# Moving three value loads, four low parts of weights and the turn of one expert group's tokens in a fused attention and mixture-of-experts kernel

## Chip, cores and metric

The kernel runs on one core of a Trainium2 chip. The metric is the device time of one execution in microseconds (us); lower is better. A difference of under 1% is taken as no change.

## What is computed

A block-sparse attention is followed by a mixture of experts with one expert per token. The attention has 4 batches, 8 heads, 768 positions and 64 columns per head, in blocks of 32 positions. A block of queries sees its neighbours, the first and the last block, and three sampled blocks:

```
scores = where(mask, scale * q @ k.T, -1e9)
attn   = exp(scores - max) / (sum + 1e-9);  x = attn @ v        # 3072 tokens of 512
logits = x @ w_gate + modality_bias[modality_id];  e = argmax(logits)
out[e == i] = gate_w * (relu(x @ w1[i]) @ w2[i])                # w1 512x1024, w2 1024x512
```

Everything is float32. Products in the expert part are made of two parts: a number is kept as a rounded high part and the low part that is left (number minus high part), and a product is three matmuls: high by high, high by low, low by high.

## The kernel before

**Attention.** The queries of the first and last block are worked densely, all others in 22 tiles of 128 tokens (two halves of 11), each a batch pair with two blocks of queries. Tiles pass through a software pipeline whose steps are written out in order per engine (a manual schedule): scores (`scores`, L560), mask and maximum (L568), exponentials (L576), transposes (L585), copies to SBUF (`copied`, L590, tiles named `at`), sums over shared values (L607), sums over a tile's own sampled values (`weigh_own`, L616), division (`divide`, L461 to L463), and routing of the tokens (`turned`, `gate`, `route`, `rank`). The sampled values of a tile come by `fetch_own` (L548) with two calls of three loads of 128 KB each, issued on SP. `VG` holds where in the pipeline each call stands: the first at tick +9, place 6, the second at tick +10, place 3. `VS_SOON` and others place the copies of shared values (L530 on POOL).

**Experts.** Tokens are gathered by expert in groups of 256. There are twelve full groups and a half one here. Groups 0 and 1 are "early": they hold tokens of the first 16 and 18 tiles of 128 and run while attention ends (`early_groups`, a generator that is stepped once per part of a tick, so that its instructions are interleaved with the last attention work in a fixed order). A group has eight weights of 128x1024, numbered 8g to 8g+7; four for the first layer (`up`, L811 to L813, 96 matmuls), four for the second (`down`, L826 to L828, 48 matmuls). Each weight is loaded to a staging buffer (`fetch`, L738 to L745, on SP), rounded on ACT (L749), and its low part is made by one subtraction (`split`, L752) on VectorE (DVE), except for the numbers in `POOL_SPLITS`, which are made on GpSimd (POOL). There are five staging buffers, so weight n+5 can be fetched only when the low part of weight n is made. The first few weights of the early groups use three of the buffers only.

**Turning tokens.** A group's rows come by two indirect loads on POOL (`gather`, L763). They must be transposed, and split in high and low parts `xh`, `xl`. There are two ways. `column`, used for groups 0 to 2, turns two of the four columns per call with four TensorE transposes into PSUM (L770), then ACT copies the high part (L776) and DVE subtracts it from the PSUM tile (L777). From group 3 on the rows go another way: POOL takes the 16-bit halves of each number apart (`apart`, L786, two copies, after two tiny copies L781), SP issues one DMA transpose (`turn_halves`, L790), POOL puts the halves together again (`together`, L795, two copies), and `halve` makes the high part on ACT (L804, twice) and the low part on DVE (L805, twice) from SBUF. This way uses three buffers taken from the `at` tiles.

**Order around the change.** Each engine runs its instructions strictly in the order written. In the second layer of group 0, f counts from 0 to 7 and each f is two steps of the generator. Between these steps stand the last routing instructions on DVE (L316 to L389) and the chain that numbers all groups (`finish`, L1176 to L1238, then `rows_of`, L1077 to L1103), whose result L1079 releases the gathers of groups 2 and 3. `relu` (L818 on ACT, L819 on DVE) ends a first layer. `give` (L843 to L847) scales and scatters a group's output.

The columns of group 1 are turned by `columns(1)` at the end of f = 3 and f = 7.

Of the kernel before, what the change touches and what calls it, by code (L numbers as in the profile page):

```python
# [9 lines left out]
F32 = mybir.dt.float32  # L10
# [4 lines left out]
U16 = mybir.dt.uint16  # L15
# [6 lines left out]
P = 128  # L22
# [49 lines left out]
VS = (11, 7)  # L72
VS_SOON = (8, 7)
VG = ((9, 6), (10, 3))

DENSE_IN = ((19, 14, 30), (49, 38, 44))
Q_IN = 22
# [2 lines left out]
XD = (7, 7)  # L80
TAIL = 7
EVAC_DVE = ()
POOL_SPLITS = (7, 15, 16, 21)

TICKS = (6, 9, 12)
DOWN0 = ((9, 5), (9, 7), (14, 7), (12, 9), (13, 9), (13, 9), (17, 9), (15, 10))
# [5 lines left out]
def attention_moe(ctx, tc, kD, qD, qH, v0, v1, blocks, modality, w_gate, bias, w1, w2, out):  # L92
# [30 lines left out]
    with ExitStack() as actx:  # L123
# [623 lines left out]
        def split(n, eng=None, rest=None):  # L747
            h, l, s = wh[n % NRING], wl[n % NRING], staged(n)
            nc.scalar.copy(h, s)  # L749

            def low():
                (eng or (nc.gpsimd if n in POOL_SPLITS else nc.vector)).tensor_tensor(l, s, h.bitcast(F32), ALU.subtract)  # L752

            if rest is None:
                low()
            else:
                rest.append(low)
# [25 lines left out]
        def apart(g):  # L783
            keep_share(g, nc.gpsimd.tensor_copy)
            for t in range(2):
                nc.gpsimd.tensor_copy(halves[0][:, t * GT * 4:(t + 1) * GT * 4].rearrange("p (n f) -> p n f", n=2),  # L786
                                      xg[2 * (g % 2) + t][:, 0:HD].bitcast(U16).rearrange("p (f n) -> p n f", n=2))

        def turn_halves():
            nc.sync.dma_start_transpose(halves[1].rearrange("p (k r) -> p k r", r=P), halves[0])  # L790

        def together(g):
            bits = halves[2].rearrange("p (c t n) -> p n c t", n=2, t=GT)
            for t in range(2):
                nc.gpsimd.tensor_copy(bits[:, :, :, t * P:(t + 1) * P],  # L795
                                      halves[1][:, t * GT * 4:(t + 1) * GT * 4].rearrange("p (n c r) -> p n c r", n=2, c=4))

        def halve(g):
            whole = halves[2].bitcast(F32)
            for n in range(2):  # L800
                h = xh[g % 2][:, 2 * n:2 * n + 2, :].rearrange("p a b -> p (a b)")
                l = xl[g % 2][:, 2 * n:2 * n + 2, :].rearrange("p a b -> p (a b)")
                x = whole[:, n * 2 * GT:(n + 1) * 2 * GT]
                nc.scalar.copy(h, x)  # L804
                nc.vector.tensor_tensor(l, x, h.bitcast(F32), ALU.subtract)  # L805
# [46 lines left out]
        def early_groups():  # L852
            now = {"fetch": 0, "split": 0, "gather": 0, "column": 0, "half": 0}
            lows = []

            def load(nf, ns, slow=False):
                while True:
                    f, p = now["fetch"], now["split"]
                    if p < ns and p < f:
                        split(p, rest=lows if slow else None)  # L860
                        now["split"] += 1
                        if slow:
                            return
                    elif f < nf and f - NSTG < p and (f < 8 * NEAR or known):
                        if slow or now["half"]:
                            fetch(f, now["half"])
                            now["half"] ^= 1
                        else:
                            fetch(f)
                        now["fetch"] += not now["half"]  # L870
                        if slow:
                            return
                    else:
                        return

            def rows(g):
                if now["gather"] == g and ready[g] and (g != 1 or tail[1]) and (g or settled() and 2 * NM - 1 in shared):
                    if g == 1:
                        expert_slots(8)
                    gather(g)  # L880
                    if g == NEAR:
                        gather(g + 1)
                    now["gather"] += 1

            def columns(g):
                for n in range(2):
                    if now["column"] == 2 * g + n and now["gather"] > g:
                        column(g, n, bank())
                        now["column"] += 1
                        return  # L890

            expert_slots(0)
            tick, wait = 0, 0
            while not tail[0]:
                while lows:
                    lows.pop()()
                rows(0)
                if now["gather"]:
                    wait += 1
                    if wait > 8:  # L900
                        columns(0)
                p = sum(tick >= x for x in TICKS)
                load(p + 2, p, True)
                tick += 1
                yield "tick"
            while lows:
                lows.pop()()
            expert_slots(2, 5, 6, 7)
            while now["column"] < 2:
                rows(0)  # L910
                columns(0)
            load(10, 5)
            for k in range(4):
                o = bank()
                for c in range(4):
                    for f in (2 * k, 2 * k + 1):
                        up(0, c, f, o)
                    rows(1)
                    yield
                relu(k, o)  # L920
            o = [bank() for _ in range(2)]
            for f in range(8):
                load(*DOWN0[f])
                for t in range(2):
                    down(0, f, t, o[t])
                    rows(1)
                    yield
                if f in (3, 7):
                    columns(1)
            while not tail[1]:  # L930
                yield
            rows(1)
            for t in range(2):
                give(0, t, o[t])
            while now["column"] < 4:
                columns(1)
            o = [bank() for _ in range(4)]
            for c in range(4):
                load(*UP1[c])
                for f in range(8):  # L940
                    up(1, c, f, o[f // 2])
                    if f % 2:
                        rows(2)
                        yield
            for k in range(4):
                relu(k, o[k])
            turned_low.append(True)
            o = [bank() for _ in range(2)]
            for f in range(8):
                load(*DOWN1[f])  # L950
                for t in range(2):
                    down(1, f, t, o[t])
                    rows(2)
                    yield
                if f in (5, 6):
                    columns(2)
            while not ready[2]:
                yield
            rows(2)
            for _ in range(3):  # L960
                at_ = work.tile([P, 16, 2, 32], F32, name="at", bufs=NAT)
                halves.append(at_.rearrange("p a b c -> p (a b c)").bitcast(U16))
            apart(NEAR + 1)
            for t in range(2):
                give(1, t, o[t])
            load(22, 17)
            while now["column"] < 6:
                columns(2)
            load(22, 20)
# [307 lines left out]
        def side(t, f, place=7):  # L1277
            work_at.setdefault((t, place), []).append(f)
# [58 lines left out]
        for g in range(2 * NM):  # L1337
            half, m = divmod(g, NM)
            t = at["s", half, m, 0, 0]
            kl = lambda m=m, half=half: q_load(m, half)  # L1340
            qp = lambda m=m, half=half: share_k(m, half)
            vl = lambda m=m, half=half: fetch_v(m, half)
            vg = [lambda m=m, half=half, n=n: fetch_own(m, half, n) for n in range(2)]
            if g < 2:
                loads.update({f"kl{g}": kl, f"qp{g}": qp, f"vl{g}": vl, "vs1": lambda: share_v(1, 0), **{f"v{n}{g}": vg[n] for n in range(2)}})
                continue
            kt = last(g - 2) + KL[0]
            pt = max(kt, t + QP[0])
            vt = last(g - 2) + VL[0]
            side(kt, kl, KL[1])  # L1350
            side(pt, qp, QP[1])
            side(vt, vl, VL[1])
            if m:
                vs = VS_SOON if g >= 2 * NM - 2 else VS
                side(last(g - 2) + vs[0], lambda m=m, half=half: share_v(m, half), vs[1])
            for n in range(2):
                side(last(g - 2) + VG[n][0], vg[n], VG[n][1])

        st, done = {}, set()

# [164 lines left out]
```

## Time and profile before

| what | value |
| --- | --- |
| median of 3 runs | 528.4 us (523.78 to 529.88) |
| profiled execution | 526.72 us, its span 524.9 us |
| PE busy | 503.9 us, 96% of the span |
| DVE, ACT, POOL busy | 388.5, 336.8, 285.5 us |
| HBM traffic | 225 GB/s over the span |

Busy time of an engine counts its instructions, not the waits. "PE" is TensorE's matmuls, "PEld" its weight loads, "SPq" the queue of SyncE, from which nearly all loads are issued. In a row of a timeline the two numbers ahead are the start and the length in us; a bracket at the end tells how long the engine stood idle before, and what released it. Rows of a kind that follow each other are merged, with their count behind an x. The profiled execution is one run; it took 1.7 us less than the median of the three.

### The profile page before, as it was taken

What the parts mean: (1) busy time and instruction counts of PE and PEld (TensorE: products, weight loads), DVE (VectorE), ACT (ScalarE), POOL (GpSimd) and SP (SyncE); (2) the same over time, 40 slices, a digit from 0 to 9 for tenths busy, and PEclk for the clock granted to TensorE, in tenths of its full rate; (3) what the DMA queues carried; (4) which work ended last, traced back from release to release, by engine and by line L of the source; (5) the groups of instructions that cost most, each with busy time, mean ns of one, the idle gap of its engine ahead of it and who ended that gap; (6) DMA issues with size and microseconds to landing.
All of it is one profiled execution on the core that took longest, in us unless ns stands there. A gap on an engine that the chain in (4) does not pass through costs nothing.

```text
span 524.9 us, 18927 instructions
## 1 busy us (share of the span) xinstructions
PE 503.9 (96%) x7218; PEld 423.9 (81%) x7218; DVE 388.5 (74%) x1119; ACT 336.8 (64%) x771; POOL 285.5 (54%) x532
## 2 busy tenths in 40 slices
PE   7999999999999999889999999999999999999995
PEld 5677676767778777778889798988989899898984
DVE  6885698677688899967996657667677675867663
ACT  4789787978878978844545646546465555655562
POOL 6788685576458884321376466654517254263313
PEclk9999999999999999999999999999999999999999
DMA  8986896979655689965877969987969788797740
GB/s 295 336 247 195 225 274 188 251 223 254 179 179 160 196 227 253 259 201 194 270 249 258 327 187 327 312 240 257 276 229 296 211 274 249 250 284 229 248 161 24
DMA packets 70101, 124.61 MB, mean 237 GB/s; under 512 B 28529, under 2 KB 28786, under 8 KB 70002
## 3 DMA queue, kind: packets, MB, share of 16 engines
q1 hardware_dynamic: 65904, 110.19, 70.1%
q0 software_dynamic: 4096, 13.12, 7.2%
q8 instruction: 59, 0.97, 0.8%
q14 instruction: 40, 0.33, 0.2%
q10 hardware_dynamic: 2, 0.00, 0.0%
HBM read 105.44 MB, written 12.86 MB: 225 GB/s over the span
## 4 chain that ended last, share of the span: by engine, by line
PE 37%; issue 21%; DMA 18%; DVE 11%; POOL 10%; ACT 1%; POOLq 1%; SPq 0%; DVEq 0%; ACTq 0%
DMA slot<-x_d,gi 11%; PE bank L560 6%; PE bank L585 6%; POOL out L847 4%; POOL at L786 4%; PE bank L616 3%; DVE y L568 3%; PE bank L607 3%; DMA out<-slot,si 3%; PE bank L454 2%; PE bank L400 2%; PE bank L633 2%; DMA at<-at 2%; PE bank L432 2%; PE bank L811 1%
## 5 line engine op out<-in xcount | busy, mean ns | idle before, releaser
L752 DVE TENSOR_TENSOR slot<-slot 128x1024 fp32r<-128x1024 f32 x99 | 135.1, 1373 | 69.9 <-ACT slot L749 63.0
L749 ACT CAST slot<-slot 128x1024 fp32r<-128x1024 f32 x104 | 108.2, 1049 | 95.8 <-PE bank L812 45.8
L811 PE MATMUL bank<-slot 128*128 128x256 f32 x384 | 108.4, 282 | 0.0
L813 PE MATMUL bank<-slot 128*128 128x256 f32 x384 | 107.7, 281 | 0.0
L812 PE MATMUL bank<-slot 128*128 128x256 f32 x384 | 107.6, 280 | 0.0
L576 ACT ACTIVATE a<-y,mn 128x256 f32<-128x256 f32 x176 | 89.1, 514 | 11.6 <-DVE mn L568 11.5
L828 PE MATMUL bank<-slot 128*128 128x512 f32 x192 | 75.9, 396 | 0.8 <-DVE slot L819 0.8
L826 PE MATMUL bank<-slot 128*128 128x512 f32 x192 | 75.9, 395 | 0.4 <-ACT slot L818 0.4
L827 PE MATMUL bank<-slot 128*128 128x512 f32 x192 | 76.0, 396 | 0.0
L811 PEld LDWEIGHTS bank<-slot 128*128 128x128 f32 x384 | 72.2, 188 | 0.6
L812 PEld LDWEIGHTS bank<-slot 128*128 128x128 f32 x384 | 72.1, 188 | 0.4
L813 PEld LDWEIGHTS bank<-slot 128*128 128x128 f32 x384 | 72.2, 188 | 0.0
L568 DVE CUSTOM_DVE_ANT_1 y<-bank,smask 128x256 f32<-128x256 f32 x176 | 66.3, 417 | 0.5
L847 POOL DMA_INDIRECT out<-slot,si x20 | 26.5, 1325 | 73.6 <-ACT slot L843 70.4
L505 POOL COPY slot<-slot 128x128 f32 x264 | 64.2, 295 | 0.0
L530 POOL TENSOR_SCALAR slot<-slot 32x1024 f32<-32x1024 f32 x40 | 41.9, 1048 | 34.5 <-PE bank L616 14.2
L590 ACT COPY at<-bank 128x512 f32<-128x512 f32 x88 | 50.8, 579 | 7.8 <-PE bank L585 7.7
L585 PE MATMUL bank<-ident,a 128*128 128x128 f32 x352 | 52.0, 280 | 0.8 <-ACT a L422 0.5
L560 PE MATMUL bank<-slot,q_raw 64*32 64x256 f32 x1408 | 49.8, 382 | 0.6 <-issue 0.6
L828 PEld LDWEIGHTS bank<-slot 128*128 128x128 f32 x192 | 36.1, 188 | 10.0 <-DVE slot L819 1.7
L827 PEld LDWEIGHTS bank<-slot 128*128 128x128 f32 x192 | 36.0, 188 | 8.5 <-DVE slot L752 0.4
L826 PEld LDWEIGHTS bank<-slot 128*128 128x128 f32 x192 | 36.1, 188 | 8.3 <-ACT slot L818 0.6
(313 smaller groups left out, 901.6 us busy)
## 6 DMA issues: line engine op xcount, KB each, us to landing
slot<-w SPq DMA_DIRECT2D x100, 512.0 KB
slot<-v SPq DMA_DIRECT2D x180, 128.0 KB
x_d<-xr SPq DMA_DIRECT2D x22, 256.5 KB
q_raw<-qH SPq DMA_DIRECT2D x22, 256.0 KB
slot<-v SPq DMA_DIRECT2D x16, 256.0 KB
slot<-kD SPq DMA_DIRECT2D x13, 256.0 KB
slot<-v SPq DMA_DIRECT2D x4, 768.0 KB
slot<-w SPq DMA_DIRECT2D x10, 256.0 KB
```

What stands on the lines that cost most here:

```text
L560: nc.tensor.matmul(sp[u][32 * pr:32 * pr + 32, b * 256:(b + 1) * 256], lhsT=q[r, b * NPAIR + pr, n, :], rhs=kv[r, s0:s0 + 8, b, pr, :], st ...
L568: nc.vector.tensor_tensor_reduce(y[:, u, :].rearrange("p (s f) -> p s f", s=8), sp[u][:, b * 256:(b + 1) * 256].rearrange("p (s f) -> p s ...
L576: nc.scalar.activation(a[:, u, :], y[:, u, :], AF.Exp, bias=mn[:, u:u + 1], scale=-1.0, accum_out=total[:, u:u + 1])
L585: nc.tensor.transpose(tp[:, k:k + P], a[:, u, c * P:(c + 1) * P], ident)
L749: nc.scalar.copy(h, s)
L752: (eng or (nc.gpsimd if n in POOL_SPLITS else nc.vector)).tensor_tensor(l, s, h.bitcast(F32), ALU.subtract)
L811: nc.tensor.matmul(o, lhsT=h[:, fs], rhs=xh[g % 2][:, c, :], start=c == 0 and f % 2 == 0, stop=False)
L812: nc.tensor.matmul(o, lhsT=h[:, fs], rhs=xl[g % 2][:, c, :], start=False, stop=False)
L813: nc.tensor.matmul(o, lhsT=l[:, fs], rhs=xh[g % 2][:, c, :], start=False, stop=c == 3 and f % 2 == 1)
L826: nc.tensor.matmul(o, lhsT=hh[0][:, f, ts_], rhs=h[:, fs], start=f == 0, stop=False)
L827: nc.tensor.matmul(o, lhsT=hh[0][:, f, ts_], rhs=l[:, fs], start=False, stop=False)
L828: nc.tensor.matmul(o, lhsT=hl[f // 4][:, f % 4, ts_], rhs=h[:, fs], start=False, stop=f == 7)
```

## The change

The last tile's second three loads of sampled values move from tick +10, place 3 to tick +9, place 7, one place behind its first three. The list `POOL_SPLITS` goes, so that the low parts of weights 7, 15, 16 and 21 are made on VectorE. (The half group's own split on POOL stays.) Group 1 is turned by the way of the later groups: `apart` at the end of f = 0 of group 0's second layer, the DMA transpose at the end of f = 1, `together` at the end of f = 4, `halve` for all four columns at the end of f = 7. The three buffers for it are taken there, and no longer after group 1.

```diff
 VG = ((9, 6), (10, 3))
+VG_LAST = ((9, 6), (9, 7))
...
-POOL_SPLITS = (7, 15, 16, 21)
...
-                (eng or (nc.gpsimd if n in POOL_SPLITS else nc.vector)).tensor_tensor(l, s, h.bitcast(F32), ALU.subtract)
+                (eng or nc.vector).tensor_tensor(l, s, h.bitcast(F32), ALU.subtract)
...
-                if f in (3, 7):
-                    columns(1)
+                if f == 0:
+                    for _ in range(3):
+                        at_ = work.tile([P, 16, 2, 32], F32, name="at", bufs=NAT)
+                        halves.append(at_.rearrange("p a b c -> p (a b c)").bitcast(U16))
+                    apart(1)
+                if f == 1:
+                    turn_halves()
+                if f == 4:
+                    together(1)
+                if f == 7:
+                    halve(1)
+                    now["column"] = 4
             while not tail[1]:
                 yield
             rows(1)
             for t in range(2):
                 give(0, t, o[t])
-            while now["column"] < 4:
-                columns(1)
...
-            for _ in range(3):
-                at_ = work.tile([P, 16, 2, 32], F32, name="at", bufs=NAT)
-                halves.append(at_.rearrange("p a b c -> p (a b c)").bitcast(U16))
             apart(NEAR + 1)
...
             for n in range(2):
-                side(last(g - 2) + VG[n][0], vg[n], VG[n][1])
+                spot = (VG_LAST if g == 2 * NM - 1 else VG)[n]
+                side(last(g - 2) + spot[0], vg[n], spot[1])
```

## Rows read from the trace of the kernel before

**Rows 1.** The page's first part: busy time, share of the span and number of instructions.

```profile
PE 503.9 (96%) x7218; PEld 423.9 (81%) x7218; DVE 388.5 (74%) x1119; ACT 336.8 (64%) x771; POOL 285.5 (54%) x532
```

**Rows 2.** Who PE waited for, from 225 us to the end: us in total, times, longest us.

```profile
PE bank L616 <- DMA slot<-v: 1.7, 1, 1.7
PE bank L828 <- DVE slot L819: 0.8, 2, 0.6
```

**Rows 3.** Timeline of SP's queue, 216 to 224 us: the loads of the last tile's values (L548) and of halves of a weight (L738).

```profile
216.67 1.33 SPq L548 DMA_DIRECT2D slot<-v  x3
219.78 0.90 SPq L738 DMA_DIRECT2D slot<-w  x2
220.87 1.42 SPq L548 DMA_DIRECT2D slot<-v  x3
```

**Rows 4.** Timeline of PE at the end of the last attention tile and in the first products of group 0.

```profile
227.65 1.09 PE L616 MATMUL bank<-slot,at 128*32 128x64 f32 x62 [1.68 <-DMA slot<-v]
228.68 0.39 PE L811 MATMUL bank<-slot 128*128 128x256 f32 x1
...
231.90 0.28 PE L813 MATMUL bank<-slot 128*128 128x256 f32 x1
```

**Rows 5.** Timelines of ACT and DVE in the same stretch: the arrival of group 0's rows, and the low parts of weights 3 and 4.

```profile
224.24 0.19 ACT L781 COPY share<-slot 128x1 f32<-128x1 f32 x1 [1.34 <-DMA slot<-x_d,gi_e]
...
229.62 2.35 DVE L752 TENSOR_TENSOR slot<-slot 128x1024 fp32r<-128x1024 f32 x2
```

**Rows 6.** Timeline of PE around the turn of group 1's first two columns (L770, four transposes at 248.72), and group 1's first product with a low part of the tokens (L812 at 255.40).

```profile
248.49 0.39 PE L828 MATMUL bank<-slot 128*128 128x512 f32 x1
...
249.40 0.40 PE L827 MATMUL bank<-slot 128*128 128x512 f32 x1
249.63 0.40 PE L828 MATMUL bank<-slot 128*128 128x512 f32 x1
...
255.40 0.28 PE L812 MATMUL bank<-slot 128*128 128x256 f32 x1
```

**Rows 7.** Timeline of POOL from 229 us (the second of group 1's gathers, and two instructions of routing), with the time to landing of all gathers from the view of line L763 (min/median/max).

```profile
230.83 1.98 POOL L763 DMA_INDIRECT slot<-x_d,gi_e  x1 [0.30 <-issue]
239.05 0.86 POOL L389 TENSOR_SCALAR lhs<-iota_f,rlo,code 128x128 f16<-128x128 f32 x1 [6.23 <-DVE rlo L379]
247.72 2.04 POOL L389 TENSOR_SCALAR lhs<-iota_f,rlo,code 128x128 f16<-128x128 f32 x1 [7.81 <-DVE rlo L379]
...
DMA to landing us min/median/max: 5.4/6.5/8.4
```

**Rows 8.** The views of single lines: number of instructions, their shortest, median and longest time in ns, first and last start in us.

```profile
L752 POOL TENSOR_TENSOR slot<-slot x5: 2402/2417/2427, 249.7 to 511.9; 128x1024 fp32r<-128x1024 f32 x5
L786 POOL COPY at<-slot x20: 1035/1044/2047, 279.1 to 474.5; 128x1024 uint16<-128x1024 uint16 x20
L790 SPq DMA_TRANSPOSE at<-at x10: 2757/4046/6766, 284.6 to 481.1; - x10
L795 POOL COPY at<-at x20: 1351/1388/2320, 293.4 to 495.8; 128x1024 uint16<-128x1024 uint16 x20
L805 DVE TENSOR_TENSOR slot<-at,slot x20: 677/686/1525, 300.4 to 503.7; 128x512 fp32r<-128x512 f32 x20
```

**Rows 9.** Timelines of DVE and POOL at two places where both work in SBUF: one instruction of the routing (L324) under two POOL instructions, and low parts of weights (L752) under the pair of L795.

```profile
161.95 2.17 POOL L530 TENSOR_SCALAR slot<-slot 32x1024 f32<-32x1024 f32 x2
162.03 0.99 DVE L324 SCALAR_TENSOR_TENSOR eq<-dl,desc 128x16 f32<-128x16 f32 x1
...
399.93 2.67 POOL L795 COPY at<-at 128x1024 uint16<-128x1024 uint16 x2
400.70 4.07 DVE L752 TENSOR_TENSOR slot<-slot 128x1024 fp32r<-128x1024 f32 x2 [1.61 <-ACT slot L749]
```

**Rows 10.** Timelines of DVE and PE: the first instruction of the last routing chain (L316), and the ranking matmul (L356) that waits for the chain's end.

```profile
240.92 0.16 DVE L316 TENSOR_REDUCE mx<-lg 128x2 f32<-128x16 f32 x1
...
241.98 0.18 PE L356 MATMUL bank<-oh,upper 128*128 128x8 bf16 x1 [0.21 <-DVE oh L329]
```

**Rows 11.** Busy time in the stretch from the low part of weight 5 to the last L777 of group 1 (stretch, its length, PE, PEld, DVE, ACT, POOL, granted clock, DMA share, GB/s), and three rows of DVE's timeline in it.

```profile
244.77:256.10 11.33, 11.33 (x56) 8.96 (x55) 10.80 (x27) 5.06 (x9) 4.41 (x2) 1.00 0.50 179
...
248.00 1.22 DVE L752 TENSOR_TENSOR slot<-slot 128x1024 fp32r<-128x1024 f32 x1
249.98 0.69 DVE L777 TENSOR_TENSOR slot<-bank,slot 128x512 fp32r<-128x512 f32 x1 [0.28 <-ACT slot L776]
250.59 1.57 DVE L1188 SCALAR_TENSOR_TENSOR gh<-gh,iota_f 128x8 f32<-128x8 f32 x1
```

**Rows 12.** Timelines around PE's last stall, between the layers of group 2: PE's matmul before it and the fourth behind it, the rounding of weight 23 on ACT, and the low parts of weights 15 and 16 on POOL.

```profile
290.58 0.28 PE L813 MATMUL bank<-slot 128*128 128x256 f32 x1
...
292.96 0.40 PE L826 MATMUL bank<-slot 128*128 128x512 f32 x1
...
289.66 1.05 ACT L749 CAST slot<-slot 128x1024 fp32r<-128x1024 f32 x1 [2.26 <-DMA slot<-w]
...
270.87 4.79 POOL L752 TENSOR_TENSOR slot<-slot 128x1024 fp32r<-128x1024 f32 x2
```

**Rows 13.** Busy time behind the last matmul, which ended before 519 us (columns as in rows 11).

```profile
519.00:523.50 4.50, 0.00 (x0) 0.00 (x0) 0.47 (x1) 0.00 (x0) 1.34 (x2) 1.00 0.20 60
523.50:524.90 1.40, 0.00 (x0) 0.00 (x0) 0.00 (x0) 0.00 (x0) 0.00 (x0) 0.50 0.02 6
```

## The prediction, made before the changed kernel was run

> **What bounds the kernel.** I read the share of busy time first: TensorE is busy 96% of the span [rows 1]. The list of its waits shows what the rest is worth: from 225 us on PE waits twice for anything over a few tenths, once for the last tile's values and once between the layers of group 2 [rows 2]. Everything else there is TensorE running its own queue without a gap. So in the part that the change touches, time is won only by taking instructions off TensorE or by ending one of those two waits, and lost by any new wait in front of it. Work that DVE, ACT or POOL gain or lose counts only where PE stands behind it.
>
> **The value loads.** SP issues the first three up to 218.0, then stands before the two halves of weight 4 until 219.78, since their staging buffer is not free, and issues the second three at 220.87 [rows 3]. Issued right behind, they leave about 2.8 us earlier; the halves of weight 4, first used in group 0's second layer, come behind them. The change removes the wait of 1.68 us before L616 [rows 4]. What is late next is on DVE: the first of the pair at 229.62, the low part of weight 3, ends near 230.85 [rows 5], and the first matmul that needs it ran at 231.90 [rows 4]. So at most 1.05 us can be had here. That low part stands in DVE's order behind the turn of group 0, whose rows arrived at 224.24 [rows 5], and three loads more now travel beside that gather; if they delayed it by 0.85, only 0.2 would stay. I take 0.9 (0.2 to 1.05), since 384 KB are little beside the weights already in that queue.
>
> **The low parts.** One takes 2.4 us on POOL [rows 8] and 1.2 on DVE [rows 5].
> - Weight 7: POOL made it at 249.73, and DVE's L1188 under it took 1.57 us [rows 11], where such a small one takes about 0.2 (L316 in rows 10: 0.16). DVE is given 1.2 and gets 1.37 back. PE does not wait for it either way.
> - Weights 15 and 16: POOL starts at 270.87 and takes 4.79 for both [rows 12], behind the gathers. The fetches of weights 20 and 21 wait for these buffers, and so the whole line of loads. On DVE they are done one to three us earlier. What that is worth shows at PE's second wait: from 290.58 to the fourth matmul behind are 2.38 us, where 0.12 and three times 0.23 would do, a loss of 1.57; the relu stood behind the rounding of weight 23, which had waited 2.26 for its load [rows 12]. I take 1.5 back (0.5 to 1.57), all the more as PE comes there later (below).
> - Weight 21: nothing waits for it; nothing.
>
> **Turning group 1: what goes.** Between 248.49 and 249.40 PE did two matmuls and four transposes; at 0.23 a matmul [rows 6] the four cost 0.45, and twice that is 0.9 us off PE. ACT's and DVE's two instructions each stay (L776 and L777 become L804 and L805; L777 takes 0.69 [rows 11], L805 0.686 [rows 8]).
>
> **What comes: apart.** Group 1's second gather is issued at 230.83, rows land 5.4 to 8.4 us after an issue, and POOL is then held by L389, from 239.05 to 239.91 [rows 7]. So the two L786, 1.04 each [rows 8], run at about 240.0 to 242.1, or 0.9 earlier with PE's shift. On DVE the last routing chain starts at 240.92, and PE already waits 0.21 for its end [rows 10]; it moves with PE, and so lies under the copies. A row shows what that does: L324, in the same chain of an earlier tile, took 0.99 under POOL's L530 [rows 9], where small instructions like L316 take 0.16 [rows 10]: it waited until POOL's instruction ended. Three of the chain's five instructions are of that kind. I take 1.1 us more wait for PE at L356 (0, if copies and chain miss each other, to 2.0, both copies).
>
> **The DMA transpose** holds SP for 2.8 to 6.8 us [rows 8]. Behind it on SP stand the fetches of weights 10 and 11, needed only half way through group 1's first layer: nothing. It should land before POOL is free of its second L389, at 249.76 [rows 7]: nothing.
>
> **Together and halve.** Here I expect most of the loss. Before, the first two columns were ready at 250.67 (L777 of rows 11), well ahead of PE. Now the first product with a low part of the tokens (L812, before at 255.40 [rows 6]) needs the first L805, which stands behind everything that DVE has to do in this stretch. PE arrives at 255.40 - 0.9 + 1.1 - 0.9 = 254.7. DVE's stretch was 11.33 us long with 10.80 busy [rows 11]. Without L777 (0.61 start to start), its idle 0.28 and L1188's 1.37, with weight 7's 1.2, the first L805 starts 10.27 after the low part of weight 5, which moves by 0.2 to 244.97: at 255.24 if nothing holds DVE. But POOL runs L389 and then the pair L795 in it. Under that pair two L752, 2.35 alone [rows 5], took 4.07, 1.7 more, the first waiting through both copies [rows 9]; L389 adds some 0.5, and the small instructions wait as well. I take 2.5 (0 to 3.1). L805 then starts at 257.75 and is done at 258.4: PE stalls 3.7 us, and L812 is 3.0 us later than before.
>
> The Trainium skill ("SBUF — State Buffer", section "Who interferes with whom") says that a DVE instruction with two SBUF inputs waits only until the GpSimd instruction that came first has finished; by that the pair of L795 would cost at most 1.3 for one copy, and L812 would come 0.4 earlier. The rows show the first L752 waiting through both copies. The same section says that one with at most one SBUF input does not wait: L777, with its PSUM operand, was such a one, and L805 is not.
>
> **The sum:** -0.9 (loads) + 1.1 (chain) - 0.9 (transposes) + 3.7 (low part of the tokens) - 1.5 (group 2) = +1.5 us. Against the profiled execution, 526.72, that is 528.2; the median shown is 1.7 above that execution, which would make it 529.9. I say 529.0; this case's own range is 527 to 532.
>
> **Rivals.**
> - *The copies fall into gaps.* POOL's copies run while DVE is at instructions that don't mind, the chain is not held, and L805 starts without delay. PE arrives at L812 at 253.6, L805 ends at 254.8 (all of the stretch 0.9 earlier), so PE loses 1.2 and L812 is 0.6 earlier; with 1.0 to 1.5 from group 2 the change wins 1.6 to 2.1 us: about 525.7. For it: the median L786 of 1044 ns [rows 8] is one that nobody delayed. Against it: DVE has only 0.53 us free in its stretch [rows 11].
> - *The clock falls.* PE's new stall stands at the start of group 1; before, no stall from 225 us on was over 1.7. After the last matmul the granted clock stood at 1.00 up to 523.5 and then at 0.50, 1.2 GHz, more than 4.5 us after PE had stopped [rows 13]. If the stall at L812 grows to that, group 1's first layer starts at 1.2 GHz. No row shows how long it would stay there; it costs at least 0 and, for a whole first layer of 96 matmuls at 0.12 each (half of the 0.23 of twice as many columns), 11 us. I take 4: 533, slower. It decides from a stall of about 4.5 us, and I have 3.7. The Trainium skill ("TensorE: Matmul & The Clock Gate", section "What's actually happening") says the throttled clock is the default and activity releases it, which that fall agrees with.
> - *The moved loads bring nothing,* because they land no earlier in a full queue, or hold up the gather of group 0 by as much: 0.9 more than my forecast, 529.9.
>
> **Chances.** My forecast 0.50, gaps 0.30, clock 0.08, loads 0.12. What a measurement can tell from no change is about 1%, 5.3 us, since the three runs before spread over 6.1. No case reaches 523.1 by its own sum; with the scatter of runs I give faster 0.05, mostly out of the gaps. Slower, above 533.7, comes from half of the clock's case and the scatter on my own: 0.08. Within 1%: 0.87. The range goes from the gaps' best less scatter, 524.5, to the clock's, 533.0.
>
> **What would show it.** L616 without a wait for values, and L813 of weight 3 near 231.0, prove the loads. L316 to L329 stretched under L786 and L356 waiting about 1.3 prove the chain; if they take 0.17 each, that step is wrong. L812 at group 1's start waiting 3 to 4 us for L805 is the main step; if it waits under 1.5, the gaps' case holds. L804 waiting for L795, or L795 for the DMA transpose beyond 250, would say that the chain through POOL is the limit and not DVE. No wait between 290 and 294 proves the low parts. If PE's waits come out as here and the time still differs by over 2 us, what I took for the scatter of runs is at fault.

## The result and the profile after

The changed kernel took 529.71 us (median of 22 runs, 525.63 to 534.29), the kernel before beside it 526.67 us (22 runs, 521.87 to 530.21). The ratio is 1.0067, interval [1.0039, 1.0096]: 3.5 us more (526.67 times 0.0067), between 2.1 and 5.1. That is within 1% and inside the range, and on the slower side of zero. The range, 527 to 532, holds the three runs' median of the kernel before (528.4) as well, so that lying in it tells little. Medians here and below are of all runs of a kernel, while the ratios leave disturbed runs out.

The profiled execution took 532.55 us, 2.8 more than its median, with a span of 530.8. PE's busy time barely rose against [rows 1]:

```profile
PE 505.8 (95%) x7210; PEld 425.7 (80%) x7210; DVE 389.2 (73%) x1123; ACT 337.3 (64%) x769; POOL 274.3 (52%) x534
```

Who PE waited for, from 225 us to the end (us in total, times, longest), beside [rows 2]:

```profile
PE bank L812 <- DVE slot L805: 3.4, 1, 3.4
PE bank L607 <- POOL lhs L389: 1.5, 1, 1.5
PE bank L356 <- DVE oh L329: 1.1, 1, 1.1
PE bank L813 <- DVE slot L752: 0.4, 1, 0.4
...
PE bank L616 <- DMA slot<-v: 0.2, 1, 0.2
```

The wait for values is nearly gone (1.7 to 0.2), and the one for DVE's low part of the tokens at L812 has come. The 1.5 us at L607 lie in the attention, whose steps are not at fixed times from run to run. PE's timeline has these places (beside [rows 4, 6, 10]):

```profile
229.38 1.09 PE L616 MATMUL bank<-slot,at 128*32 128x64 f32 x62 [0.16 <-DMA slot<-v]
...
245.28 0.18 PE L356 MATMUL bank<-oh,upper 128*128 128x8 bf16 x1 [1.07 <-DVE oh L329]
...
257.58 0.28 PE L811 MATMUL bank<-slot 128*128 128x256 f32 x1
261.27 0.38 PE L812 MATMUL bank<-slot 128*128 128x256 f32 x1 [3.41 <-DVE slot L805]
```

SP issued the six value loads in one row, and the DMA transpose well ahead of need:

```profile
220.34 3.74 SPq L548 DMA_DIRECT2D slot<-v  x6
...
244.59 2.16 SPq L790 DMA_TRANSPOSE at<-at  x1
```

POOL and DVE show why L812 waits. First POOL's timeline (beside [rows 7]), then DVE's (beside [rows 11]):

```profile
242.55 2.01 POOL L786 COPY at<-slot 128x1024 uint16<-128x1024 uint16 x2
251.01 0.87 POOL L389 TENSOR_SCALAR lhs<-iota_f,rlo,code 128x128 f16<-128x128 f32 x1 [6.45 <-DVE rlo L379]
251.84 4.21 POOL L795 COPY at<-at 128x1024 uint16<-128x1024 uint16 x2
```

```profile
243.55 1.05 DVE L319 TENSOR_TENSOR dl<-lg,mx 128x16 f32<-128x16 f32 x1
...
251.30 3.54 DVE L752 TENSOR_TENSOR slot<-slot 128x1024 fp32r<-128x1024 f32 x2
254.77 1.32 DVE L1186 TENSOR_SCALAR gnum<-gcount 128x8 int32<-128x8 int32 x1
...
258.15 1.23 DVE L752 TENSOR_TENSOR slot<-slot 128x1024 fp32r<-128x1024 f32 x1
...
260.53 0.68 DVE L805 TENSOR_TENSOR slot<-at,slot 128x512 fp32r<-128x512 f32 x1
```

L319 lasts until the pair L786 ends (244.56). Under L389 and the pair L795 the two L752 lose 1.2 us (they take 2.35 alone, [rows 5]), and L1186 loses 1.15 (it took 0.16 in the kernel with the turn undone, below). L805 then comes last in DVE's order, at 260.53, and PE stands before it.

Stretches of time, with busy time and number of instructions of PE, PEld, DVE, ACT and POOL, then the granted clock, DMA share and GB/s:

```profile
257.90:261.20 3.30, 0.00 (x0) 0.00 (x0) 3.19 (x6) 2.75 (x3) 1.10 (x1) 1.00 0.42 134
261.30:262.40 1.10, 1.10 (x9) 1.10 (x10) 1.10 (x3) 0.00 (x0) 0.00 (x0) 0.99 0.95 222
262.40:265.80 3.40, 3.40 (x18) 3.40 (x17) 3.33 (x8) 0.33 (x1) 1.12 (x1) 0.50 0.75 273
265.80:270.00 4.20, 4.20 (x55) 4.16 (x54) 3.99 (x12) 1.46 (x2) 0.00 (x0) 1.00 0.48 125
```

PE does nothing for 3.3 us. It works for 1.1 us at the full clock, and then for 3.4 us at 0.50, which is 1.2 GHz: 18 matmuls there, where the stretch behind has 55 in 4.2 us. This fall is what the sum left out.

**Where the time went.** The matmuls that number group 1's rows (L1162 before, L1167 after; 18 of them, one per tile) start anywhere from 220.4 to 227.7 us in these profiles, with or without the change. So I measure in stages between matmuls of PE, worked out from their starts in each trace. S0: the first of these 18 to group 0's first product. S1: to the first of group 0's second layer (L826). S2: to group 1's second product (L812). S3: to group 1's L826. S4: to group 3's first product. S5: to group 4's L826. S6: to the last matmul. All in us:

| kernel | S0 | S1 | S2 | S3 | S4 | S5 | S6 |
| --- | --- | --- | --- | --- | --- | --- | --- |
| before | 8.31 | 14.24 | 12.49 | 11.93 | 36.11 | 33.86 | 181.36 |
| changed | 7.78 | 15.81 | 15.06 | 13.56 | 34.53 | 34.43 | 180.95 |
| changed, again | 5.39 | 16.38 | 15.04 | 13.55 | 34.54 | 34.42 | 180.94 |
| filled | 7.07 | 16.38 | 15.04 | 11.96 | 34.54 | 38.25 | 181.79 |
| turn alone | 7.38 | 15.89 | 15.79 | 13.54 | 36.79 | 34.14 | 181.49 |
| turn undone | 7.09 | 15.50 | 12.40 | 11.93 | 34.97 | 38.37 | 181.00 |
| loads alone | 5.98 | 14.74 | 12.40 | 11.93 | 35.37 | 33.86 | 181.38 |
| low parts alone | 7.07 | 14.25 | 12.40 | 11.93 | 35.84 | 33.86 | 181.95 |
| low parts, one load fewer | 6.58 | 14.24 | 12.39 | 11.90 | 34.53 | 33.86 | 181.44 |
| one load fewer | 9.61 | 14.25 | 12.40 | 11.93 | 34.81 | 33.86 | 180.92 |
| halve at f = 6 | 7.17 | 16.38 | 12.50 | 12.02 | 36.37 | 35.16 | 181.23 |
| apart early | 6.96 | 15.51 | 11.72 | 12.30 | 35.76 | 35.62 | 181.93 |
| apart early, one load fewer | 6.04 | 14.95 | 11.94 | 12.28 | 35.97 | 35.44 | 180.92 |
| the same, values not moved | 10.34 | 15.73 | 11.73 | 12.28 | 36.05 | 35.44 | 180.90 |

From S1 to S6 the changed kernel's profile is 4.4 us behind: +1.57, +2.57, +1.63, -1.58, +0.57, -0.41. S2 and S3 repeat within 0.1 where the waits are the same; S0, S4 and S5 don't: S4 was 36.11 before and 35.37 with the loads alone, which change no instruction in it. Each row is one profile.

### The profile page after: what moved, and what is told of

It reads as the page before. It is cut to its first block, busy times and chain, and to the rows that moved or that the text cites. A ratio compares the mean times of both kernels' runs of the same rounds, so it can differ in the third digit from the quotient of the medians.

```text
span 530.8 us, 18918 instructions
## 1 busy us (share of the span) xinstructions
PE 505.8 (95%) x7210; PEld 425.7 (80%) x7210; DVE 389.2 (73%) x1123; ACT 337.3 (64%) x769; POOL 274.3 (52%) x534
## 4 chain that ended last, share of the span: by engine, by line
PE 38%; issue 21%; DMA 18%; POOL 9%; DVE 9%; ACT 2%; SPq 1%; POOLq 1%; DVEq 0%; ACTq 0%
DMA slot<-x_d,gi 11%; PE bank L560 7%; PE bank L585 6%; POOL at L786 4%; POOL out L847 4%; PE bank L616 3%; PE bank L607 3%; DMA out<-slot,si 2%; PE bank L454 2%; PE bank L811 2%; PE bank L813 2%; PE bank L812 2%; PE bank L400 2%; PE bank L633 2%; DVE slot L752 2%
## 5 line engine op out<-in xcount | busy, mean ns | idle before, releaser
L752 DVE TENSOR_TENSOR slot<-slot 128x1024 fp32r<-128x1024 f32 x103 | 142.6, 1394 | 66.7 <-ACT slot L749 64.6
L812 PE MATMUL bank<-slot 128*128 128x256 f32 x384 | 108.5, 282 | 3.4 <-DVE slot L805 3.4
L812 PEld LDWEIGHTS bank<-slot 128*128 128x128 f32 x384 | 72.9, 190 | 4.2 <-DVE slot L805 3.7
L828 PE MATMUL bank<-slot 128*128 128x512 f32 x192 | 75.8, 395 | 0.3 <-DVE slot L819 0.3
L826 PE MATMUL bank<-slot 128*128 128x512 f32 x192 | 75.7, 394 | 0.0
L813 PEld LDWEIGHTS bank<-slot 128*128 128x128 f32 x384 | 73.0, 190 | 0.7 <-DVE slot L752 0.7
L811 PEld LDWEIGHTS bank<-slot 128*128 128x128 f32 x384 | 73.0, 190 | 0.6
L828 PEld LDWEIGHTS bank<-slot 128*128 128x128 f32 x192 | 36.1, 188 | 9.1 <-DVE slot L819 0.7
L585 PEld LDWEIGHTS bank<-ident,a 128*128 128x128 f32 x352 | 38.7, 142 | 5.2 <-ACT a L422 0.7
L827 PEld LDWEIGHTS bank<-slot 128*128 128x128 f32 x192 | 36.0, 188 | 8.3 <-DVE slot L752 0.4
```

Of the source, the lines that this page charges most:

```text
L585: nc.tensor.transpose(tp[:, k:k + P], a[:, u, c * P:(c + 1) * P], ident)
L752: (eng or nc.vector).tensor_tensor(l, s, h.bitcast(F32), ALU.subtract)
L811: nc.tensor.matmul(o, lhsT=h[:, fs], rhs=xh[g % 2][:, c, :], start=c == 0 and f % 2 == 0, stop=False)
L812: nc.tensor.matmul(o, lhsT=h[:, fs], rhs=xl[g % 2][:, c, :], start=False, stop=False)
L813: nc.tensor.matmul(o, lhsT=l[:, fs], rhs=xh[g % 2][:, c, :], start=False, stop=c == 3 and f % 2 == 1)
L826: nc.tensor.matmul(o, lhsT=hh[0][:, f, ts_], rhs=h[:, fs], start=f == 0, stop=False)
```

## The experiments

Kernels that ran together shared their runs of the kernel before.

**The turn alone, and the turn undone.** The first is the kernel before with the new turn only. The second is the changed kernel with `columns(1)` at f = 3 and 7 again; loads and low parts stay moved.

```diff
-                if f in (3, 7):
-                    columns(1)
+                if f == 0:
+                    ...
+                    apart(1)
+                if f == 1:
+                    turn_halves()
+                if f == 4:
+                    together(1)
+                if f == 7:
+                    halve(1)
+                    now["column"] = 4
...
```

> The kernel before with the DMA transpose of group 1 alone; the loads stay late and weights 7, 15, 16, 21 stay on POOL. Theory: the turn alone makes more than the whole loss. L356 waits about 1.1, L812 3.5 to 5 us (POOL's weight 7 now stands ahead of together), the clock falls for one stretch (1.6 us), L616 waits 1.7, and the stall of group 2 is gone because PE comes later: ratio 1.008 to 1.012. Rival (the three parts only hurt together): 1.003 or less.

> Group 1 is turned on TensorE again; the moved loads and all low parts on VectorE stay. My theory (the turn alone costs time, the other two parts win it): no wait of PE at group 1's first L812, no fall of the clock there, L356 waiting about 0.2 us as before, L616 waiting under 0.3, no stall of over 0.5 us between the layers of group 2; against the kernel before -1.05 (loads) - 1.5 (group 2) = -2.5 us, a ratio of 0.995. Rival (the loads or the low parts on VectorE are what makes the changed kernel slower, by a fuller DVE queue): still 1.004 to 1.007.

The turn alone: 535.34 us, ratio 1.0093 [1.005, 1.0136], as expected. L356 waits 1.1, L812 3.5, and the clock is at half in 262.5 to 265.6. The stall of group 2, which was expected to go, stays: S4 is 36.79. So the turn makes the loss. Undone: 528.98 us, 1.0025 [0.9993, 1.0056], where 0.995 was expected. L812's wait and the fall in group 1 are gone, but loads and low parts win nothing that the times show. In the profile S4 gains 1.1 against before, and S5 loses 4.5. POOL's and DVE's timelines of this kernel show where:

```profile
312.62 0.96 POOL L763 DMA_INDIRECT slot<-x_d,gi  x1 [0.30 <-DMA at<-at]
313.57 2.61 POOL L795 COPY at<-at 128x1024 uint16<-128x1024 uint16 x2
```

```profile
312.91 4.31 DVE L752 TENSOR_TENSOR slot<-slot 128x1024 fp32r<-128x1024 f32 x1 [1.59 <-ACT slot L749]
317.14 2.47 DVE L819 SCALAR_TENSOR_TENSOR slot<-bank,slot 128x512 fp32r<-128x512 f32 x4
```

The same two engines in the kernel before:

```profile
313.82 3.02 POOL L795 COPY at<-at 128x1024 uint16<-128x1024 uint16 x2
```

```profile
313.13 1.23 DVE L752 TENSOR_TENSOR slot<-slot 128x1024 fp32r<-128x1024 f32 x1 [1.59 <-ACT slot L749]
```

Before, L752 took its 1.23 and POOL's pair took 3.02. Here the pair took 2.61 and L752 waited through it: 4.31. The relu L819 stands behind it and PE before L828, for 2.7 us. The clock then fell as in group 1 (stretches as above):

```profile
315.20:317.80 2.60, 0.00 (x0) 0.00 (x0) 2.60 (x3) 1.24 (x3) 0.98 (x1) 1.00 0.85 312
...
318.30:321.60 3.30, 3.30 (x10) 2.58 (x9) 2.44 (x4) 0.06 (x1) 1.55 (x3) 0.53 1.02 409
```

Wait and clock together make up nearly all of the 4.5 us that S5 has over before. It does not happen each time: with the low parts alone, S5 is 33.86 as before. The Trainium skill ("SBUF — State Buffer", section "Who interferes with whom") says that issue order decides which of the two blocks. In these records L752 begins 0.66 to 0.69 us ahead of the copies in both kernels, and the outcome differs, so they don't show the deciding order.

**The changed kernel again, and filled.** The second keeps PE busy for a part of the stall:

```diff
             for t in range(2):
                 give(0, t, o[t])
+            fill = bank()
+            for _ in range(40):
+                nc.tensor.matmul(fill[:, 0:P], lhsT=onesb, rhs=onesb, start=True, stop=True)
             o = [bank() for _ in range(4)]
```

> The changed kernel once more, on the same chip as the three others, as the measure for the filled one. Theory: 1.0067 of the kernel before's time, L812 waits 3.4 us for L805 at 257.9 us, and the clock is at half for 3.4 us from about 262.4 us. Rival (the fall of the clock was an accident of the one profiled run): the same wait and no fall behind it.

> The changed kernel with 40 spare matmuls of 128 columns (bf16, about 2.2 us in all, into a bank that nobody reads) ahead of group 1's first layer, so that PE works through most of the time in which L812 waits for L805; the rest is as changed. Theory (the stall costs twice: 3.4 us of waiting, and then a clock at half for 3.4 us, worth 1.6 us): L812 runs at the same time as in the changed kernel, its own wait is 1.0 to 1.5 us in place of 3.4, the granted clock stays at 1.00 through group 1's first layer, and the time is about 1.6 us below the changed kernel's, 0.9970 of it, 1.0035 of the kernel before's. Rival (the fall has another cause than the stall, or costs nothing): the clock falls near 262 us in spite of the filling, or the time stays at 1.0067 of the kernel before's.

Again: 531.46 us, 1.0114 [1.0058, 1.017]. L812 waited 3.39, and the stretch behind it was again at half:

```profile
258.30:261.70 3.40, 3.40 (x17) 3.40 (x18) 3.33 (x9) 0.00 (x0) 1.12 (x1) 0.52 1.00 350
```

Filled: 531.98 us, 1.0102 [1.0063, 1.0141]: not the 1.6 us less that the theory expected of the time. The stages show why. PE and the stretches behind the stall, filled:

```profile
257.83 0.36 PE L811 MATMUL bank<-slot 128*128 128x256 f32 x1
259.27 0.39 PE L812 MATMUL bank<-slot 128*128 128x256 f32 x1 [1.08 <-DVE slot L805]
```

```profile
259.30:261.80 2.50, 2.50 (x21) 2.50 (x22) 2.43 (x8) 0.03 (x1) 1.04 (x1) 1.00 1.02 343
261.80:265.20 3.40, 3.40 (x49) 3.36 (x48) 3.40 (x4) 1.05 (x1) 0.08 (x1) 1.00 0.82 235
```

S2 is the same (15.04), so L812 comes no later; the clock stays at 1.00; and S3 is 11.96 in place of 13.55. In the three profiles with a stall of 3.4 or 3.5 us here the clock fell behind it, and S3 took 13.54 to 13.56. So this stall causes this fall, and the fall costs 1.6 us. But the 1.6 us were lost again in S5 (38.25): another L752 there waited through POOL's pair, PE waited 2.6 for L819, and the clock fell behind that. That is one profile. The timed runs of the two kernels can't be told apart (the intervals overlap), and they don't say in how many runs the saved time is lost again.

**Loads alone, low parts alone.** The kernel before with `VG_LAST`, and without `POOL_SPLITS`:

> The kernel before with the three value loads moved and nothing else. Theory: L616's wait of 1.7 us goes, L813 waits for the low part of weight 3 by up to 1.0, so PE is 0.5 to 1.05 us earlier in group 0's second layer and stays so to the end: 0.998 to 0.999 of the kernel before's time. Rival (the loads hold up the gather of group 0, L770 waits for its rows by 0.8 to 1.6 us, and the gain is gone or turned round): PE at group 0's second layer within 0.3 us of before or later, 1.000 to 1.002.

> The kernel before with the low parts of weights 7, 15, 16 and 21 on DVE and nothing else. Theory: the loss of 1.6 us between the layers of group 2 goes, PE is 1.3 to 1.6 us earlier from 294 us to the end: 0.997 of the kernel before's time. Rival (given back in group 3, where a low part on DVE meets POOL's gather and L795 at the shared port, so that L819 and L828 behind it come up to 2.7 us late, or the clock takes it): the stall at 291 us is gone and one of 1 to 3 us stands between 310 and 340 us, 1.000 to 1.003.

Loads: 526.26 us, 0.9997 [0.9955, 1.0039]. Low parts: 525.78 us, 0.998 [0.994, 1.0021]. Neither is told from 1. In the first, PE's wait at the values shrinks from 1.7 to 0.2 us, and a new one for weight 3's low part comes (lines are one higher in this kernel):

```profile
PE bank L814 <- DVE slot L753: 0.2, 1, 0.2
...
PE bank L617 <- issue: 0.2, 1, 0.2
```

With the turn undone, where the values were moved as well, these were the waits ahead of group 0's second layer:

```profile
PE bank L770 <- DMA slot<-x_d,gi_e: 1.5, 1, 1.5
PE bank L813 <- DVE slot L752: 1.0, 1, 1.0
```

S0 and S1 together, less 0.86 where the chain waits (1.07 against 0.21), are 20.7 to 22.7 in eight profiles with the loads moved, 22.0 in the mean, and 20.8 to 23.9 in five without, 22.2 in the mean (the last kernel of the table is not among them: the clock fell in its S1). The 0.2 between the means is far below that spread. Much of the spread is the gather of group 0, for which PE waits 0 to 1.6 us (L770) with and without the move. Weight 3's low part stands in DVE's order behind the turn of that gather (4.1 to 4.3 us from the first L777 to it in eleven profiles, up to 5.4 in the others), so PE meets it whatever the values do.

The low parts alone left the stall in group 2: S4 was 35.84, 0.3 less than before and no less than with the loads alone, and PE still waited 0.6 us there for the relu. ACT's timeline (lines one lower) still has the two waits for weights that the kernel before has there (2.94 us, and the 2.26 of [rows 12]):

```profile
284.69 1.05 ACT L748 CAST slot<-slot 128x1024 fp32r<-128x1024 f32 x1 [2.49 <-DMA slot<-w]
288.22 1.05 ACT L748 CAST slot<-slot 128x1024 fp32r<-128x1024 f32 x1 [2.48 <-DMA slot<-w]
```

**One load fewer.** Weight 22 is loaded twice into the same buffer, by a `load` in group 1's second layer and again by `ahead(16)`. Two kernels leave the second load out, with and without the low parts on DVE:

```diff
-            if n + LOOK_D < 8 * NGMAX and n not in (8 * NG, 8 * NG + 1):
+            if n + LOOK_D < 8 * NGMAX and n not in (8 * NEAR, 8 * NG, 8 * NG + 1):
```

> The kernel before with the low parts on DVE, and without the second of the two loads of weight 22 (512 KB that are loaded twice into the same buffer, at the end of group 1 and again at the start of group 2). Theory (with PE on time the loss in group 2 comes from the line of weight loads, not from POOL's two low parts): from group 1's second layer to group 3's first PE takes 34.5 to 35.0 us, where the kernel with the low parts alone took 35.8 and the kernel before 36.1, and ACT's roundings wait less than 1 us for loads there; 0.996 of the kernel before's time. Rival (POOL's low parts or another engine set it): 35.8 as with the low parts alone, 0.998.

> The kernel before without the second load of weight 22, the low parts of weights 15 and 16 still on POOL. Theory (the line of loads is the limit): from group 1's second layer to group 3's first 34.7 to 35.3 us in place of 36.1, 0.997 of the kernel before's time. Rival (POOL's 4.8 us for two low parts are the limit): 36 us as before, 1.000.

With low parts: 525.87 us, 0.9993 [0.9958, 1.0028]. Without: 530.15 us, 1.0024 [0.9977, 1.0071]; its S0 of 9.61 has a wait of 2.3 for values. The times settle nothing, the stage says more: S4 is 34.53 and 34.81, in one profile each, where no kernel with two loads and PE on time came under 34.97. Even with the low parts on POOL, 512 KB less bring S4 to within 0.3 of the changed kernel's. The roundings in the kernel with both, at the places of the two rows above, wait for PE and no longer for a load:

```profile
288.23 1.05 ACT L748 CAST slot<-slot 128x1024 fp32r<-128x1024 f32 x1 [1.75 <-PE bank L811]
291.08 1.05 ACT L748 CAST slot<-slot 128x1024 fp32r<-128x1024 f32 x1 [1.80 <-PE bank L811]
```

The span from which the prediction took its 1.57 us tells more than S4: from the last matmul of group 2's first layer to the fourth of its second. It is 0.80 to 0.81 us in all four kernels of the table with one load fewer, and in the changed, repeated and filled ones. It is 2.38 before, 2.23 with the turn alone, 2.10 with the low parts alone, 1.90 with halve at f = 6, 1.47 with the loads alone, 1.24 with the turn undone and 0.93 with apart early. So in these profiles group 2's stall is the line of loads being late, and POOL's low parts are only one of the things that keep it late.

**Other places for the turn.** Three kernels move the parts of the turn apart from their collisions: `halve` at f = 6; `apart` in group 0's first layer (k = 2), the transpose at f = 0 and `halve` at f = 5; and the latter with one load fewer.

```diff
-                if f == 7:
+                if f == 6:
                     halve(1)
```

> The changed kernel with halve(1) one f earlier, so that on DVE it stands ahead of weight 9's low part, L1213 and L1216 (1.23 + 0.18 + 1.11 us). Theory (DVE's order is the limit at L812): the wait at L812 falls from 3.4 to about 1.0 us, the clock stays at full, together 2.4 + 1.6 us less than the changed kernel: ratio to before about 0.999. Rival (the chain through POOL, DMA transpose and L804 is the limit): the wait stays above 2.5 and the ratio at 1.005 to 1.007.

> The changed kernel with apart(1) before POOL's first L389 (at k = 2 of group 0's first layer), the DMA transpose at the end of f = 0, together as it was, halve(1) at the end of f = 5. Theory: L786 ends before the routing chain starts, so L319 takes 0.17 and L356 waits 0.2 as before (1.07 in the changed kernel); L805 starts before PE needs it, so L812 waits under 0.5; no fall of the clock. Against the changed kernel 1.0 + 3.2 + 1.6 = 5.8 us less, ratio to before about 0.994. Rival (two-input DVE instructions and POOL copies cost the same wherever they stand): 1.000 or more.

> The kernel of e3_apart_early (whole change, apart in group 0's first layer, halve at f = 5) with weight 22 loaded once. Theory: as there, 11.7 us from group 0's second layer to group 1's second matmul and no fall of the clock, and from group 1's second layer to group 3's first 34.5 to 35.0 us in place of 35.8: 0.995 of the kernel before's time. Rival (given back behind group 3, where DVE's low parts meet POOL's copies): 35.5 us or more from group 3's first layer to group 4's second, and 0.998 or more.

Halve at f = 6: 531.73 us, 1.0057 [1.0019, 1.0094]. S2 is down from 15.06 to 12.50 (L812 waits 0.9), and no fall follows, yet S1, S4 and S5 took 3.1 us more than in the changed kernel, in a profile of the longest of its twelve executions (537.35). Apart early: 529.71 us, 0.9976 [0.9942, 1.001]. L356 waits 0.2 as before, and S2 is 11.72, 0.8 under before: the turn without its collisions is worth about what the transposes cost, four of them taken off PE twice. S3 to S5 then give back 1.8 against before (PE waited 1.5 us for L805 at the start of group 4's first layer). With one load fewer: 529.15 us, 1.0029 [0.9988, 1.007]; PE waited 2.2 us in two parts for L819. The first part, 0.85 us at the start of group 1's second layer, lies in S4, which is 35.97 where 34.5 to 35.0 was expected. The last with the value loads where they were:

> The changed kernel with apart in group 0's first layer (k = 2), the transpose at f = 0 and halve at f = 5, the value loads where they were before, and weight 22 loaded once. Theory: PE waits 0.2 us at L356 and under 0.5 at group 1's L812, 11.7 us from group 0's second layer to group 1's second matmul (12.5 before, 15.1 changed), no fall of the clock there, 34.5 to 35.0 us from group 1's second layer to group 3's first, so 2 us less than before: 0.996. Rival (what is won is given back behind group 3, where DVE's low parts meet POOL's copies): group 3's first layer to group 4's second over 35.5 us (33.9 before), 0.999 or more.

529.02 us, 1.0035 [0.9992, 1.0078]. PE waited 2.7 us for the values, the clock fell behind that, and L819 was late as in the one before; S4 was 36.05. The expected ratios of these four kernels, 0.994 to 0.999, were all missed. No version beats the kernel before by what can be measured.

## Why the prediction was right, and where it was wrong

- **Value loads, -0.9: wrong, -0.2 at most that can be read, and that can't be told from nothing.** The wait went as said. The step that failed is "at most 1.05 us can be had here ... I take 0.9": I took the place of weight 3's low part from one profile, while it follows the gather of group 0, which moves by more than the gain. The rival of loads that bring nothing came close, by DVE's order and not by holding up the gather: L770 waits as long without the move.
- **The chain, +1.1: right,** 0.86 more wait. One instruction, L319, took the whole of it, as L324 did in [rows 9].
- **Transposes, -0.9: right.** PE was 3.30 behind at group 0's L826 and 2.38 at group 1's first product.
- **L812's wait, 3.7: right,** 3.41, and 3.39 in the repeat. DVE's block was 2.35 where I took 2.5. The limit was DVE's order and not POOL: L804 ended its wait for L795 at 256.09, 4.4 us ahead of L805.
- **Group 2, -1.5: right in size, the cause only half seen.** S4 fell by 1.58. Alone, the low parts brought 0.3 at most, since the loads stayed late; with PE delayed by the turn and the low parts still on POOL, S4 was 36.79 (turn alone). In the changed kernel PE comes later, so that the loads have caught up, and POOL no longer holds them. My "all the more as PE comes there later" was nearer to a condition than to an addition. That both together are needed is not shown: it is read from one profile each, and without the delay at L812 the turn undone had only 0.4 of the 1.57 left, apart early 0.1 (PE had lost 0.8 before it there, waiting for L819).
- **The clock: the step that failed.** The rival was right in mechanism and wrong in where it decides. "It decides from a stall of about 4.5 us" came from the one row of the end of the kernel, [rows 13], and 4 us was a guess for its price. It came behind 3.41, and cost 1.6 us. The Trainium skill ("TensorE: Matmul & The Clock Gate", section "Terms") puts the penalty at the throttled time multiplied by the share of clock withheld. For the 3.4 us at half of the rows above that makes 1.7, an estimate that the 1.6 bears out.

The sum, +1.5, with the clock's 1.6 and 0.7 for the loads added, is +3.8. The chain and the wait at L812 take 0.5 off (0.24 and 0.29), which makes 3.3, against 3.5 measured. That the time said, 529.0, lay near 529.71 is in part luck: the three runs that I started from had a median 1.7 us above that of the 22. The change cost more than twice the 1.5 us of the sum.

## What to carry to other kernels

A stall of the bottleneck engine can have two prices, the wait and the clock behind it; a rival that rests on the clock should be given its chance by stalls seen in the middle of a trace, not by the end of the kernel alone. A low part that POOL gives up is worth only what the next late thing leaves, and when a stall vanishes after a change that also delays the engine, the delay may be what took it away. Where DVE instructions with two SBUF operands stand between POOL's long copies and a relu, allow for a wait through the whole copy pair (4.31 us in place of 1.23 here). In these kernels each way to take one collision away left one in another group.

## What the runs showed that I had not expected

From 225 to 345 us the six stalls of PE at 2.6 us or more (3.4, 3.4 and 3.5 at L812; 2.7 and 2.6 at L828; 2.7 at the values) were each followed within 1.2 us by some 3.4 us at 1.2 GHz, and none of the stalls up to 2.3 us was (2.3 and 1.7 at the values, 1.6 and 1.5 at L770 in three kernels). Forty matmuls of no use, in the filled kernel, were enough to keep the clock up.

Over the whole traces the length of a stall does not settle it. With halve at f = 6, PE stood for 2.7 us before L616, from 218.4 us on, and the clock stayed at 1.00 until after the last matmul. Here is that wait, the longest of two (us in total, times, longest), and below it the page's row of the granted clock: 40 slices of 13 us, in tenths, where a 9 is 90% or more:

```profile
PE bank L616 <- issue: 3.1, 2, 2.7
...
PEclk9999999999999999999999999999999999999998
```

The same row of the changed kernel has two falls. The second is the one behind L812; the first, at 122.4 us, came 1.1 us behind a stall of only 1.5:

```profile
PEclk9999999998999999999899999999999999999999
```

Four more stalls of 1.6 to 1.9 us ahead of 125 us, in other profiles, were followed by such a fall, and stalls of that length at the same places were not (1.5 us at 120.0 with the loads alone, 1.9 at 7.7 in the repeat). What decides besides the length is open.

A single L752 took 1.23 or 4.31 us at the same place, with its start 0.28 or 0.29 us behind that of POOL's L763. What decides which engine gets through is open. It wasn't tried to keep L795 away from L819 in group 3, which would tell whether the gains of the earlier turn last to the end.
